# Summing the two column sets of the last half tile one behind the other, and storing the first during the second

## The chip, the cores and the metric

The kernel runs on one NeuronCore of a Trainium2 chip. The metric is the time of one execution on the device, in microseconds. Before the change the median of three runs is 351.83 us (351.61 to 352.06). A profile is one further execution, recorded by the hardware profiler: its span runs from the first to the last recorded instruction, and its own time is the span and what lies around it.

Names of engines: PE (matrix products), DVE and ACT (vector and scalar work, both used here for copies out of PSUM), POOL and SP (here they only issue DMAs and pass signals on). SP, ACT and POOL each have a queue of their own for DMAs; DMAs issued from SP and ACT have their descriptors made by hardware, those from POOL by software.

## The reference

Attention with normalised q and k, and a multiplicative feed-forward on its output. With x the attention's output, reshaped to 3584 tokens of 768 values:

```python
q_n, k_n = (rmsnorm(q, g_q), rmsnorm(k, g_k))
scores = scale * np.matmul(q_n, k_n.transpose(0, 1, 3, 2))
attn = np.exp(scores - np.max(scores, axis=-1, keepdims=True))
attn = attn / (np.sum(attn, axis=-1, keepdims=True) + 1e-09)
x = np.matmul(attn, v)                 # batch 8, heads 12, 448 positions, head size 64
a = x @ w1
b = x @ w2
h = a * b @ w3
out = h @ w_out                        # (3584, 768), float32
```

## The kernel before

The kernel multiplies w3 and w_out together once (`w34s`), so that the end of the feed-forward is a single product, (a * b) @ w34. Batches are taken in pairs, 896 tokens each, in seven tiles of 128 tokens; `abT` holds the transposed a * b of a pair, with 8 blocks of 128 rows (`CF` = 8). Six of the last pair's seven tiles are ordinary passes (`ffn2_pair`): 64x64 products into two PSUM banks, one copy of 128x768 into `half`, and two stores of 64 rows, for the last pair one from SP and one from ACT.

The last tile of all is different. `do_last` makes it in two halves of 64 tokens (x = 0, then x = 1). In a half, the 768 output columns are cut in four pieces of 192 (`w`): `nh` picks the left or right 384 columns and becomes the upper or lower 64 partitions of the result, `c` picks the first or second 192 of these and becomes the PSUM bank `z + c`. So one bank holds a column set: the piece `c` of both column halves. For each of the 8 blocks there are four matmuls of 192 columns (two sets, two halves), 32 in a half tile. In the kernel before, all four of a block come before the next block, so both banks are complete at the end. Then DVE copies bank `z` and ACT copies bank `z + 1` into a buffer that is free by then (`qk_bufs[0]`, called `qk_sb` in the profile), and when both are done, SP stores the left 384 columns of the 64 rows and ACT the right ones (96 KB each).

The order of everything is made by a planner (`Planner`). It is a simulation in Python: each operation is a `Job` with a cost, a key and conditions for when it may start; the planner takes the earliest job, emits its instruction, and so fixes the order in each engine's queue. The numbers in `add(...)` (an engine, an estimated cost, a key, `needs`) and the times `at` are the planner's own estimates: they set the order of emission, not when an instruction runs. What runs when is set by semaphores, which the framework adds from the data that each instruction reads and writes. The framework also gives each DMA one of eight semaphores ("lanes") for hardware-made descriptors or one of eight for software-made ones; an issue first waits until the DMA that last used its lane has landed.

`hand_over` uses signals on SP or POOL between two parts of an accumulation; in the last 80 us these are the only instructions of POOL. At the end of the program (line 1426 in the profile) SP waits for every DMA semaphore, each engine drains, and the engines meet in a barrier that POOL leads.

Of the kernel before, what the change touches and what calls it, by code (L numbers as in the profile page):

```python
# [20 lines left out]
SEM = 0.05  # L21
TO_ENGINE = 0.23
TO_ENGINE_WIDE = 0.45
# [22 lines left out]
class Planner:  # L46
# [11 lines left out]
    def add(self, *args, **kw):  # L58
        self.jobs.append(Job(*args, **kw))
# [136 lines left out]
def kernel(  # L196
# [13 lines left out]
    nc = tc.nc  # L210
# [3 lines left out]
    HP = NP // 2  # L214
# [9 lines left out]
    CF = DFF // 128  # L224
    NH = DM // 2
# [50 lines left out]
    w34s = const.tile([128, CF, DM], BF, name="w34s")  # L276
# [43 lines left out]
    ps_all = psum.tile([NP, 8, 512], FP, name="ps_all")  # L320
# [9 lines left out]
    free, add = plan.free, plan.add  # L330
# [20 lines left out]
    xT, abT = {}, {}  # L351
# [11 lines left out]
    def copy_on(engine, out, in_, by=None):  # L363
        if engine == "ACT":
            nc.scalar.activation(  # L365
                out=out, in_=in_, func=AF.Copy, scale=1.0 if by is None else by
            )
        elif by is not None:
            nc.vector.tensor_scalar(out=out, in0=in_, scalar1=by, scalar2=None, op0=MULT)
        else:  # L370
            nc.vector.tensor_copy(out=out, in_=in_)  # L371
# [252 lines left out]
    def into(m):  # L624
        extra = DRAIN if mode[0] != m else 0.0
        mode[0] = m
        return extra

    def pass_us(n):
        return n / 2400 + 0.0025  # L630
# [421 lines left out]
    def out_rows(bp, t, x):  # L1052
        bb, j = divmod(2 * t + x, NJ)
        r0 = (2 * bp + bb) * S
        return out[r0 : r0 + S].rearrange("(p j) n -> j p n", j=NJ)[j]
# [9 lines left out]
    def do_last(t, z):  # L1065


        x = last_x[0]
        last_x[0] += 1
        bp, tl = B // 2 - 1, NT - 1  # L1070
        c0 = tl * 128 + HP * x
        w = NH // 2
        for fi in range(CF):
            for c in range(2):
                for nh in range(2):
                    n0 = nh * NH + c * w
                    nc.tensor.matmul(  # L1077
                        out=ps_all[HP * nh : HP * nh + HP, z + c, 0:w],
                        lhsT=abT[bp][:, fi, c0 : c0 + HP],
                        rhs=w34s[:, fi, n0 : n0 + w],  # L1080
                        start=(fi == 0), stop=(fi == CF - 1),
                        tile_position=(0, HP * nh), skip_group_check=True,
                    )
        took = 2 * CF * pass_us(w) + into("l")
        bank_at[z] = bank_at[z + 1] = INF
        spare = qk_bufs[0].rearrange("p w x j d -> p (w x j d)")
        o_sb = spare[:, x * NH : (x + 1) * NH].rearrange("p (z n) -> p z n", z=1)
        ends = []

        def store(nh):  # L1090
            eng = nc.scalar if nh else nc.sync
            eng.dma_start(
                out=out_rows(bp, tl, x)[:, nh * NH : (nh + 1) * NH],
                in_=o_sb[HP * nh : HP * nh + HP, 0],
            )

        def done(e):
            ends.append(e + SEM)
            if len(ends) == 2:
                for nh in range(2):  # L1100
                    add(
                        "ACT" if nh else "SP", 0.6, -500.0 + nh,
                        lambda nh=nh: store(nh), needs=[lambda: max(ends)],
                    )

        for c, (e, us) in enumerate((("DVE", 0.27), ("ACT", 0.25))):
            add(
                e, us, -500.0,
                lambda e=e, c=c: copy_on(
                    e, o_sb[:, 0, c * w : (c + 1) * w], ps_all[:, z + c, 0:w]  # L1110
                ),
                needs=[lambda: t + took + TO_ENGINE_WIDE - 0.16], done=done,
            )
        return took

    def push_ffn(b):
# [137 lines left out]
    def pe_try(t, r):  # L1254
# [47 lines left out]
        if next_pv[0] == NQ and not waiting and not pairs and last_x[0] < 2 and two is not None:  # L1302
            if tile_at(B // 2 - 1, NT - 1) + SEM <= r:
                return do_last(t, two)
# [10 lines left out]
    with tc.manual_schedule():  # L1315
# [41 lines left out]
        def spread():  # L1357
# [14 lines left out]
            done=lambda t: consts_at.update(g=t + SEM) or bank_at.__setitem__(6, t + SEM),  # L1372
# [9 lines left out]
        for name in POOL_ORDER:  # L1382
            what, x = name[0], int(name[1])
# [9 lines left out]
            else:  # L1393
                dst, src, key = (w1s, moe_w1, "w1") if what == "a" else (w2s, moe_w2, "w2")
# [36 lines left out]
```

## Time and profile before

| | us |
|---|---|
| median of three runs | 351.83 |
| lowest, highest | 351.61, 352.06 |
| profiled execution, its own time | 351.65 |
| its span | 349.7 |
| PE busy in the span | 342.6 (98%) |
| ACT busy | 259.9 (74%) |
| DVE busy | 210.2 (60%) |
| POOL busy | 76.8 (22%) |
| last matmul ends (by the chain of waits) | 345.7 |
| last store issued | 346.14 |

The granted PE clock is 0.999 throughout. Times in the profile count from the start of the span. "Line op out<-in" names a group by the line of the kernel that made it and by the tiles that it writes and reads; L371 and L365 are the lines of the copy helper on DVE and ACT, L1077 is the matmul of `do_last`, L1092 its stores, L1018 the stores of the ordinary last tiles, L420 the loads of v from POOL, and L881 the ordinary passes. "Idle before <-" gives how long an engine stood idle before an instruction and what it waited for. Engines with a q (SPq, ACTq, POOLq) are the engines' queues: issues of DMAs and waits there don't count as busy time.

### The profile page before, as it was taken

What the parts mean: (1) busy time and instruction counts of PE and PEld (TensorE: products, weight loads), DVE (VectorE), ACT (ScalarE), POOL (GpSimd) and SP (SyncE); (2) the same over time, 40 slices, a digit from 0 to 9 for tenths busy, and PEclk for the clock granted to TensorE, in tenths of its full rate; (3) what the DMA queues carried; (4) which work ended last, traced back from release to release, by engine and by line L of the source; (5) the groups of instructions that cost most, each with busy time, mean ns of one, the idle gap of its engine ahead of it and who ended that gap; (6) DMA issues with size and microseconds to landing.
All of it is one profiled execution on the core that took longest, in us unless ns stands there. A gap on an engine that the chain in (4) does not pass through costs nothing.

```text
span 349.7 us, 16194 instructions
## 1 busy us (share of the span) xinstructions
PE 342.6 (98%) x7374; PEld 221.3 (63%) x7374; DVE 210.2 (60%) x296; ACT 259.9 (74%) x372; POOL 76.8 (22%) x134
## 2 busy tenths in 40 slices
PE   8999999999999999999999999999999999999995
PEld 4766656657665766656666575676665656666674
DVE  5379377997989679986669678575633221222100
ACT  4779979979999999998699898667876842222122
POOL 8376720204020520132050111403130000000000
PEclk9999999999999999999999999999999999999999
DMA  8999999589999997984998789834590014000054
GB/s 194 235 283 192 233 300 253 108 174 260 187 232 216 176 260 178 222 220 62 217 248 175 169 135 265 182 54 64 113 167 8 4 47 116 27 2 2 4 170 150
DMA packets 68488, 55.11 MB, mean 158 GB/s; under 512 B 45060, under 2 KB 62372, under 8 KB 68420
## 3 DMA queue, kind: packets, MB, share of 16 engines
q1 hardware_dynamic: 49440, 35.33, 43.3%
q0 software_dynamic: 18048, 16.92, 27.8%
q10 hardware_dynamic: 932, 1.84, 1.4%
q8 instruction: 57, 0.93, 1.1%
q14 instruction: 11, 0.09, 0.1%
HBM read 46.66 MB, written 11.01 MB: 165 GB/s over the span
## 4 chain that ended last, share of the span: by engine, by line
PE 85%; ACT 8%; DVE 3%; issue 2%; DMA 1%; ACTq 0%; SPq 0%
PE ps_all L881 62%; PE ps_all L779 12%; PE ps_all L692 8%; ACT P L714 3%; PE ps_all L758 2%; ACT half L714 1%; ACT Pr L714 1%; DVE qks L507 1%; ACT sq L477 1%; DMA qk_sb<-in_q_dram 1%; PE ps_all L1077 1%; PE ps_all L1136 1%; DVE w34s L371 1%; ACT w_outs L714 1%; ACT w34s L365 0%
## 5 line engine op out<-in xcount | busy, mean ns | idle before, releaser
L714 ACT ACTIVATE P<-ps_all 128x896 bf16<-128x896 f32 x114 | 99.9, 918 | 11.0 <-PE ps_all L692 10.5
L420 POOL DMA_DIRECT2D v_sb<-in_v_dram x96 | 57.2, 623 | 175.9 <-PE ps_all L692 93.0
L881 PE MATMUL ps_all<-xT,w1s 64*64 64x448 bf16 x1536 | 88.1, 349 | 0.0
L881 PE MATMUL ps_all<-xT,w2s 64*64 64x448 bf16 x1536 | 87.3, 349 | 0.0
L881 PE MATMUL ps_all<-w34s,abT 64*64 64x384 bf16 x1728 | 80.6, 323 | 0.0
L365 ACT ACTIVATE half<-ps_all 128x896 bf16<-128x896 f32 (+1 forms) x35 | 30.7, 877 | 50.2 <-PE ps_all L881 50.2
L962 DVE TENSOR_TENSOR abT<-ps_all,half 128x896 bf16<-128x896 f32 x32 | 34.8, 1088 | 51.5 <-PE ps_all L881 49.9
L881 PEld LDWEIGHTS <-abT 64*64 64x64 bf16 x1728 | 52.8, 107 | 19.0 <-issue 0.4
L881 PEld LDWEIGHTS <-w2s 64*64 64x64 bf16 x1536 | 46.6, 107 | 25.3
L881 PEld LDWEIGHTS <-w1s 64*64 64x64 bf16 x1536 | 46.5, 107 | 25.2
L692 PE MATMUL ps_all<-qkT 64*64 64x448 bf16 x672 | 60.6, 352 | 0.6 <-DVE abT L962 0.3
L484 DVE TENSOR_REDUCE ssq<-sq 128x14 f32<-128x896 f32 (+1 forms) x50 | 51.0, 1040 | 12.8 <-ACT sq L477 12.8
L507 DVE TENSOR_TENSOR qks<-qk_sb,al 128x448 bf16<-128x448 f32 x96 | 55.7, 617 | 2.9 <-ACT al L496 2.8
L477 ACT ACTIVATE sq<-qk_sb 128x896 f32<-128x896 f32 (+1 forms) x50 | 45.2, 920 | 1.8 <-DMA qk_sb<-in_q_dram 1.5
L821 DVE TENSOR_TENSOR xT<-ps_all,r 128x448 bf16<-128x448 f32 x48 | 27.5, 616 | 13.5 <-ACT r L802 9.9
L692 PEld LDWEIGHTS <-qkT 64*64 64x64 bf16 x672 | 22.0, 106 | 14.2 <-issue 5.1
L881 PE MATMUL ps_all<-w_outs,w3T 64*64 64x384 bf16 x512 | 25.1, 323 | 0.8 <-DVE w3T L371 0.5
L779 PE MATMUL ps_all<-P,v_sb 128*32 128x448 bf16 x456 | 25.3, 352 | 0.0
L714 ACT ACTIVATE w_outs<-ps_all 128x896 bf16<-128x896 f32 x24 | 21.2, 917 | 3.8 <-PE ps_all L692 3.6
L779 PEld LDWEIGHTS <-v_sb 128*32 128x32 bf16 x592 | 16.1, 97 | 12.5 <-issue 0.8
L714 ACT ACTIVATE Pr<-ps_all 128x896 bf16<-128x896 f32 x24 | 22.2, 924 | 1.0 <-PE ps_all L692 0.9
L371 DVE COPY half<-ps_all 128x768 f32<-128x768 f32 x14 | 13.4, 957 | 13.9 <-PE ps_all L881 11.3
(65 smaller groups left out, 215.2 us busy)
## 6 DMA issues: line engine op xcount, KB each, us to landing
out_dram<-half SPq DMA_DIRECT2D x48, 192.0 KB, 3.8
qk_sb<-in_q_dram SPq DMA_DIRECT2D x15, 448.0 KB, 4.8
qk_sb<-in_k_dram SPq DMA_DIRECT2D x15, 448.0 KB, 5.6
v_sb<-in_v_dram POOLq DMA_DIRECT2D x48, 64.0 KB, 4.5
v_sb<-in_v_dram POOLq DMA_DIRECT2D x48, 48.0 KB, 4.6
qk_sb<-in_q_dram POOLq DMA_DIRECT2D x5, 448.0 KB, 11.9
qk_sb<-in_k_dram POOLq DMA_DIRECT2D x5, 448.0 KB, 12.2
w3s<-in_moe_w_dram POOLq DMA_DIRECT2D x8, 256.0 KB, 6.7
```

The source lines that it names most:

```text
L365: nc.scalar.activation(out=out, in_=in_, func=AF.Copy, scale=1.0 if by is None else by)
L371: nc.vector.tensor_copy(out=out, in_=in_)
L420: nc.gpsimd.dma_start(out=v_bufs[i % 4][p0 : p0 + HP, g::2, 0 : j1 - j0].rearrange("p h j d -> p h (j d)"), in_=src[:, g::2, j0:j1].rearra ...
L477: nc.scalar.activation(out=s["sq", t][:, x0:x1], in_=src[:, t, x0:x1], func=AF.Square)
L484: nc.vector.tensor_reduce(out=s["ssq"][:, t, x0:x1], in_=s["sq", t][:, x0:x1], axis=AX, op=ADD)
L507: nc.vector.tensor_tensor(out=s["qks"][:, t, :, x], in0=src[:, t, x], in1=s["alpha"][:, t, x].unsqueeze(2).broadcast_to([NP, NJ, D]), op=MULT,
L692: nc.tensor.matmul(out=sc[HP * c : HP * c + HP, u, 0:S].rearrange("p (j s) -> p j s", j=NJ), lhsT=qkT[u * D : (u + 1) * D, 1, j, cols], rh ...
L714: lambda: nc.scalar.activation(out=dst, in_=sc[:, :, 0:S], func=AF.Exp),
L779: nc.tensor.matmul(out=ps_all[hd * HALF : (hd + 1) * HALF, z, 0:S], lhsT=value_weights(i, hd, j, kind), rhs=s["P"][:, hd, j, :] if j < NF ...
L821: lambda: nc.vector.tensor_tensor(out=xT[b][:, 2 * m + kind - 1, :], in0=ps, in1=s["r"], op=MULT),
L881: mm = nc.tensor.matmul(out=ps_all[64 * h : 64 * h + 64, p.bank + z, 0 : p.n], lhsT=lhsT[64 * r : 64 * r + 64, 64 * h : 64 * h + 64], rhs= ...
L962: nc.vector.tensor_tensor(out=abT[bp][:, f0 : f0 + 2, odd * S : (odd + 1) * S], in0=ps_all[:, z : z + 2, 0:S], in1=a_sb[b, f0], op=MULT,)
```

## The change

Only `do_last` changes, and only for the second half (x = 1). The 32 matmuls are sorted by column set: 16 for `c = 0` over all 8 blocks, then 16 for `c = 1`. The copies and stores are made by a new function `finish`, called once per group of columns. For x = 0 it is called once, with both copies and the same two stores as before. For x = 1 it is called twice: the first set is copied by DVE and stored from SP (left part) and POOL (right part); the second set is copied by ACT and stored from SP and ACT. Each of the four stores has 64 rows of 192 columns, 48 KB. The planner's time `at` of the first set is earlier by the time of 8 of the 16 pairs.

```diff
-        for fi in range(CF):
-            for c in range(2):
-                for nh in range(2):
...
+        steps = [(fi, c) for fi in range(CF) for c in range(2)]
+        for fi, c in sorted(steps, key=lambda y: y[1]) if x else steps:
+            for nh in range(2):
...
-        def store(nh):
-            eng = nc.scalar if nh else nc.sync
+        def store(nh, n0, n1, eng):
             eng.dma_start(
-                out=out_rows(bp, tl, x)[:, nh * NH : (nh + 1) * NH],
-                in_=o_sb[HP * nh : HP * nh + HP, 0],
-            )
...
+                out=out_rows(bp, tl, x)[:, nh * NH + n0 : nh * NH + n1],
+                in_=o_sb[HP * nh : HP * nh + HP, 0, n0:n1],
+            )
+
+        def finish(n0, n1, parts, at, queues):
+            ends = []
+
+            def done(e):
+                ends.append(e + SEM)
+                if len(ends) == len(parts):
+                    for nh, (name, eng) in enumerate(queues):
+                        add(
+                            name, 0.6, -500.0 + nh,
+                            lambda nh=nh, eng=eng: store(nh, n0, n1, eng),
+                            needs=[lambda: max(ends)],
+                        )
+
+            for e, us, m0, m1 in parts:
+                add(
+                    e, us, -500.0,
+                    lambda e=e, m0=m0, m1=m1: copy_on(
+                        e, o_sb[:, 0, m0:m1], ps_all[:, z + m0 // w, m0 % w : (m1 - 1) % w + 1]
+                    ),
+                    needs=[lambda: at], done=done,
+                )
+
+        at = t + took + TO_ENGINE_WIDE - 0.16
+        ends_on = (("SP", nc.sync), ("ACT", nc.scalar))
+        if x:
+            finish(0, w, (("DVE", 0.27, 0, w),), at - CF * pass_us(w), (ends_on[0], ("POOL", nc.gpsimd)))
+            finish(w, NH, (("ACT", 0.25, w, NH),), at, ends_on)
+        else:
+            finish(0, NH, (("DVE", 0.27, 0, w), ("ACT", 0.25, w, NH)), at, ends_on)
         return took
```

More of the change, by code (lines that the diff above doesn't have):

```diff
@@ L1072, in do_last @@
         w = NH // 2
-        for fi in range(CF):
-            for c in range(2):
-                for nh in range(2):
[L1076 to L1082, printed above, removed]
-                    )
+        steps = [(fi, c) for fi in range(CF) for c in range(2)]
+        for fi, c in sorted(steps, key=lambda y: y[1]) if x else steps:
+            for nh in range(2):
+                n0 = nh * NH + c * w
+                nc.tensor.matmul(
+                    out=ps_all[HP * nh : HP * nh + HP, z + c, 0:w],
+                    lhsT=abT[bp][:, fi, c0 : c0 + HP],
+                    rhs=w34s[:, fi, n0 : n0 + w],
+                    start=(fi == 0), stop=(fi == CF - 1),
+                    tile_position=(0, HP * nh), skip_group_check=True,
+                )
         took = 2 * CF * pass_us(w) + into("l")
@@ L1087, in do_last @@
         o_sb = spare[:, x * NH : (x + 1) * NH].rearrange("p (z n) -> p z n", z=1)
-        ends = []
-        def store(nh):
-            eng = nc.scalar if nh else nc.sync
+        def store(nh, n0, n1, eng):
             eng.dma_start(
-                out=out_rows(bp, tl, x)[:, nh * NH : (nh + 1) * NH],
-                in_=o_sb[HP * nh : HP * nh + HP, 0],
-            )
[L1097 to L1113, printed above, removed]
+                out=out_rows(bp, tl, x)[:, nh * NH + n0 : nh * NH + n1],
+                in_=o_sb[HP * nh : HP * nh + HP, 0, n0:n1],
+            )
```

## The prediction

> **What bounds the kernel now.** I read the page first (span and busy shares), then the chain that ended last, and then the last ten microseconds, since all edits lie there. PE is busy 98% of the span; nothing in the change adds or takes a matmul, and the reordered ones are the last on PE. So only the tail after PE can move. The chain of waits over the end:
>
> ```profile
> 4 pieces in order of time: start us, us, what
> 335.93 6.99 PE ps_all L881 x172
> 342.92 2.78 PE ps_all L1077 x64
> 345.70 0.01 issue
> 345.71 0.36 DVE qk_sb L371
> ```
>
> It ends in a copy at 346.07, yet the span is 349.7: 3.6 us follow in which no compute engine works. The timeline of the end says what starts there (start, duration, engine; an SPq or ACTq row is an issue):
>
> ```profile
> 342.85 2.83 PE L1077 MATMUL ps_all<-w34s,abT 128*64 128x192 bf16 x64
> ...
> 344.39 0.36 DVE L371 COPY qk_sb<-ps_all 128x192 f32<-128x192 f32 x1 [15.86 <-PE ps_all L1077]
> 344.52 0.33 ACT L365 ACTIVATE qk_sb<-ps_all 128x192 f32<-128x192 f32 x1 [0.58 <-PE ps_all L1077]
> ...
> 345.71 0.36 DVE L371 COPY qk_sb<-ps_all 128x192 f32<-128x192 f32 x1 [0.96 <-PE ps_all L1077]
> 345.72 0.33 ACT L365 ACTIVATE qk_sb<-ps_all 128x192 f32<-128x192 f32 x1 [0.87 <-PE ps_all L1077]
> 346.14 0.49 ACTq L1092 DMA_DIRECT2D out_dram<-qk_sb  x1
> ```
>
> The last issue is at 346.14. The DMA answer for 340 to 349.7 gives 2.4 us to landing for SP's last store and 2.6 for ACT's: the end of data is 346.14 + 2.61 = 348.75. Then comes the program's own ending, line 1426:
>
> ```profile
> L1426 SPq EVENT_SEMAPHORE  x12: 17/28/28, 346.6 to 349.7; - x12
> L1426 POOLq EVENT_SEMAPHORE  x4: 17/17/17, 349.0 to 349.6; - x4
> L1426 POOLq DRAIN  x3: 46/101/2518, 340.5 to 349.5; - x3
> L1426 ACTq DRAIN  x2: 8/316/625, 346.7 to 349.2; - x2
> ```
>
> SP waits for all DMA semaphores (until 348.83), drains, and signals; POOL collects the engines' signals at 348.995 and 0.75 us of barrier follow to 349.75. The reader should see the third row: POOL drains three times, and the first, at 340.45, lasted 2.518 us. Today it is over at 342.97, six microseconds before POOL is needed. How full the DMA engines are in between:
>
> ```profile
> 346.20:347.40 1.20, 0.00 (x0) 0.00 (x0) 0.00 (x0) 0.00 (x0) 0.00 (x0) 1.00 0.76 272
> 347.40:348.30 0.90, 0.00 (x0) 0.00 (x0) 0.00 (x0) 0.00 (x0) 0.00 (x0) 1.00 0.68 208
> ```
>
> The last but one number is the DMA share: 0.76, then 0.68. So the end is set by latency from the last issue, with some queueing.
>
> **What the skill says.** (1) The Trainium skill, "PSUM — Partial Sum Buffer", Terms: two engines must not touch the same bank and quadrant at once. The two column sets lie in banks z and z+1, so the first may be copied while the second is summed. The trace agrees for other banks: the copies at 344.39 and 344.52 run while PE sums the next half. (2) "DMA: Bandwidth & Descriptors", Issuing engines are not separate DMA queues: stores of SP, ACT and POOL share 16 engines and interleave, so a third queue brings no bandwidth. (3) The same page, Specifications: first byte about 1 us after a software-generated (POOL) issue, 0.6 for SP and ACT. In the trace the first packets of the last SP store begin at 347.4, 1.25 us after the issue's start, 0.8 after its end; POOL's v loads in quiet stretches (issues at 236.9, 252.2, 258.6) show 1.3 to 2.0 us from the start. It agrees that POOL is slower. (4) "Perfetto Trace Analysis", Sequencer-only Instruction: a DRAIN's recorded time begins when its waits are met. So the 2.518 us is execution, not a wait. No page says what POOL does in it.
>
> **The change part by part.**
>
> *Order of sums.* 32 matmuls stay 32, with the same 32 weight loads. Pairs start every 0.0825 us in the trace of before. The first set's last pair moves from the 15th place to the 8th, 7 x 0.0825 = 0.58 us earlier; the second set's last stays where it is. Cost nothing, within 0.02 us: consecutive pairs now add into one bank, and line 881 already runs at full rate with two matmuls in one bank behind each other.
>
> *DVE copy of the first set.* Moves from 345.71 to 345.13, ends 345.49. DVE has nothing else. SP's queue has the store of the first half ahead (344.88 to 345.34), over by then.
>
> *First-set stores, two new issues.* SP: wait, then start 0.065 us after the copy as today (346.066 to 346.130), so 345.555 to 346.02 (0.467 us). That is 0.1 us before SP is needed again at 346.12; if it were later, the second store would slip by the excess, at most 0.05. POOL: in the trace's records POOL's issues whose DMA-lane semaphore came last start 0.284 us after it (thirteen cases, 0.283 to 0.290). So 345.49 + 0.285 = 345.77, and with the v loads' 0.595 us, done at 346.37. Landing is not shown for a POOL store. Low end: the fastest v load, 2.2 us, 347.97; high end: 2.9 us as at 252.2, 348.7; I take 2.6, 348.4.
>
> *Second-set copy and stores.* ACT copies at 345.72 as today, done 346.05; both stores wait for it alone instead of for two copies. Issues at 346.12, 0.015 earlier. Their size halves: 64 packets of 768 B each instead of 1,536. By the packet records, 3,072 B takes 121 ns and 1,536 B 65, so 768 B is estimated at 37: 128 x (65 - 37) / 16 = 0.22 us less work behind the last issue. In all it is 256 x 37 against 128 x 65: 0.07 us more, which with the first-set packets (2 x 0.15 us) must fit in the idle 24% of 346.2 to 347.4, 0.29 us. So 0 to 0.1 us carries over. Bounds of the gain: 0 (latency alone counts: 192 KB stores have landed in 2.5 us too) and 0.35; I take 0.25. End of data 348.5, SP ready at 348.7 instead of 348.96.
>
> *POOL's ending.* POOL's first closing DRAIN stands behind its new DMA: not at 340.45 but at 346.37 + 0.08 = 346.45 (0.08 was the gap at 340.37). With its 2.518 us it ends at 348.97, and POOL collects signals at about 349.0, against 348.995 today. The cover is gone to the last 0.03 us: what DMA gains, this DRAIN gives back. Bounds: if it is short here (the others are 0.05 and 0.10 us), it costs nothing; if it first waits for POOL's own store to land at 347.97 to 348.7 and then runs its 2.518, it ends at 350.5 to 351.2.
>
> Sum on the profiled execution: 351.65 us is 349.7 of span and 1.95 around it. SP's path -0.25, POOL's path +0.00, and the later of them counts: 349.0 - 348.995, about 0.0, so 351.65 again. The median of the three runs is 0.18 above this; added to it, the forecast is 351.8.
>
> **Rivals.**
>
> *The gain comes through* (POOL's DRAIN short, or a fixed task counted from somewhere else): the end is SP's at 348.7 and 351.83 - 0.25 = 351.6. For it: two DRAINs of 0.05 and 0.10 us on the same engine, and the one at the program's start, 0.18. Against it: those come with no DMA of POOL since the one before, the 2.518 us one does. More than 0.7 us of gain would need a landing 1.5 us after the issue, where no store shows under 2.4.
>
> *POOL's end waits for its store* (the slower side): the DRAIN sees an open software-generated transfer, holds until it has landed, and only then does its 2.518 us. From 348.995 to 350.5 or 351.2: +1.5 to +2.2 us, 353.3 to 354.0. It decides from the point where the DRAIN ends after 349.7, which is an execution of 3.3 us. For it: the only long DRAIN is the first after POOL's DMAs. Against: at 340.45 POOL's last transfer was 79 us old, so those 2.518 us can't have been such a wait.
>
> *The copy isn't early* (the DVE copy still waits for the last matmul): POOL issues at 346.07 + 0.285, DRAIN 347.0 to 349.55, +0.55 us, 352.4. Against: before, DVE starts 0.13 us ahead of ACT at 344.39, so each copy waits for its own bank.
>
> **How the numbers follow.** What a measurement of this kernel can tell from no change is about 0.2%, 0.7 us. Likeliest (a tie of the two paths): 0.50, own range 351.4 to 352.3 (the DMA and DRAIN bounds of 0.35 each way, and the runs' 0.2). Gain through: 0.20, still within 0.2%. POOL waits for its store: 0.20, slower. Copy not early: 0.05, within. The rest, 0.05: a larger gain than any row explains. To those within 0.2% I leave 0.70: 0.05 of the likeliest goes to slower, for a DRAIN some 0.8 us longer than today's. Faster 0.05, same 0.70, slower 0.25. The range must reach into the slow case to leave out no more than 2 in 10: 351.3 to 353.5.
>
> **What would show it.** In the profile after: one DVE copy near 345.1 and one ACT copy near 345.7; SP issues near 345.55 and 346.12; a POOL issue near 345.8; SP's last wait for a landing near 348.5; POOL's long DRAIN from 346.4, its first signal event at 349.0. A POOL DRAIN of 0.1 us and an end at 349.45 shows the first rival; one past 350, the second; a DVE copy at 345.7, the third. I am wrong on DMA if the last landing stays at 348.75 though the stores are halved.

## The result and the profile after

The changed kernel takes 353.33 us (median of 12 runs, 352.12 to 354.45), the kernel before 351.62 in the runs beside it: a ratio of 1.0041, 95% interval 1.0027 to 1.0055 (the two medians alone give 1.0049). It is slower, where a tie was forecast. In a second comparison (after_again below, 22 runs against 68, on one chip) it is 1.0025 (1.0010 to 1.0039).

The profiled execution took 353.76 us with a span of 352.0, against 349.7 before: 2.2 us more. Two things have to be kept apart. I call *tail* the time from the first matmul of the last tile (L1077) to the end of the span; times in the tail are counted from that matmul. Before, it starts at 342.85, so the tail is 6.90 us. After, from the timeline of the end (start, duration, engine, line):

```profile
344.30 2.83 PE L1077 MATMUL ps_all<-w34s,abT 128*64 128x192 bf16 x64
...
346.33 1.77 SPq L1090 DMA_DIRECT2D out_dram<-qk_sb  x3
...
346.59 0.36 DVE L371 COPY qk_sb<-ps_all 128x192 f32<-128x192 f32 x1 [0.39 <-PE ps_all L1077]
347.18 0.33 ACT L365 ACTIVATE qk_sb<-ps_all 128x192 f32<-128x192 f32 x1 [0.87 <-PE ps_all L1077]
347.24 0.56 POOL L1090 DMA_DIRECT2D out_dram<-qk_sb  x1 [84.81 <-PE ps_all L1077]
347.54 0.50 ACTq L1090 DMA_DIRECT2D out_dram<-qk_sb  x1
```

The tail is 7.68 us, 0.78 more. The other 1.45 us are lost before the last tile, where the instructions of PE are the same in both programs. In the table by stretches of time the first large loss shows between 139 and 147 us (the columns are the stretch, its length, the busy time of PE, PEld, DVE, ACT and POOL with the number of instructions, the granted clock, the DMA share and GB/s). The first line is of the kernel before, the second of the kernel after:

```profile
139.00:147.00 8.00, 8.00 (x184) 5.41 (x174) 7.14 (x11) 7.97 (x12) 2.38 (x4) 1.00 1.15 260
```

```profile
139.00:147.00 8.00, 7.09 (x152) 4.56 (x148) 6.04 (x9) 6.86 (x11) 2.38 (x4) 1.00 0.99 191
```

PE lost 0.91 us there, 200 us before the first changed instruction, with less DMA traffic (191 GB/s for 260). Such losses differ from run to run: over all the profiles of this study, in which the PE program up to the last tile is the same, that tile starts between 342.47 and 345.06 us. They are noise for this question, and the tail is what can be compared to a few hundredths of a microsecond: three profiles with the stores of the change have tails of 7.68, 7.73 and 7.71 us.

In the tail, the rows of the program's own ending (line 1436 after, 1426 before) and the chain of waits:

```profile
L1436 SPq EVENT_SEMAPHORE  x12: 17/28/1681, 348.1 to 351.9; - x12
L1436 POOLq EVENT_SEMAPHORE  x4: 17/17/17, 351.2 to 351.9; - x4
L1436 POOLq DRAIN  x3: 46/98/3967, 347.2 to 351.7; - x3
L1436 SPq DRAIN  x3: 7/7/7, 350.7 to 351.4; - x3
```

```profile
342.06 5.16 issue
347.22 0.58 POOLq L1436
```

The chain no longer ends in a DVE copy but in POOL's ending. POOL's first closing drain begins at 347.22, together with its issue at 347.24, and lasts 3.967 us: until 351.18. SP, which waits for all stores, is done with its waits and ready to signal at 350.80, so everybody waits 0.4 us for POOL. The stores (queue, number, size, median us from issue to landing):

```profile
out_dram<-qk_sb SPq DMA_DIRECT2D x2, 48.0 KB, 2.7
out_dram<-qk_sb POOLq DMA_DIRECT2D x1, 48.0 KB, 2.6
out_dram<-qk_sb ACTq DMA_DIRECT2D x1, 48.0 KB, 2.6
```

Stores of half the size land no sooner after their issue than the 2.4 and 2.6 us of before. So there are two questions: what POOL's drain waits for, and where the gain of the smaller stores went.

### The profile page after: what moved, and what is told of

It is laid out like the page before. It is cut to its first block, busy times and chain, and to the rows that moved or that the text cites. A ratio compares the mean times of both kernels' runs of the same rounds, so it can differ in the third digit from the quotient of the medians.

```text
span 352.0 us, 16199 instructions
## 1 busy us (share of the span) xinstructions
PE 342.6 (97%) x7374; PEld 219.5 (62%) x7374; DVE 210.3 (60%) x296; ACT 260.2 (74%) x372; POOL 77.4 (22%) x135
## 4 chain that ended last, share of the span: by engine, by line
PE 76%; ACT 11%; DVE 4%; issue 4%; DMA 3%; SPq 0%; POOLq 0%; DVEq 0%; ACTq 0%
PE ps_all L881 55%; PE ps_all L779 11%; PE ps_all L692 7%; ACT P L714 5%; DMA qk_sb<-in_k_dram 2%; PE ps_all L758 2%; DVE qks L507 2%; ACT sq L477 2%; ACT half L714 1%; ACT Pr L714 1%; DMA qk_sb<-in_q_dram 1%; PE ps_all L1146 1%; DVE w34s L371 1%; ACT w_outs L714 1%; DVE xT L821 0%
```

## The experiments

Theory A: the loss sits in the tail, and POOL's ending behind its store sets it. Rivals: the changed order of sums or copies costs time itself; the program is slower before the tail; the drain takes a fixed time from the issue, whatever the store does. Times finer than 0.1 us are read from the trace's records of instructions and of semaphores. Where no ratio is given, the kernel ran once, and only its tail is read.

**The change again.**

> The changed kernel as it is. The tail is the time from the first matmul of the last tile to the end of the span: 6.9 us before, 7.7 us in the first profile after. Theory A (the loss sits in the tail, in POOL's ending and SP's waits): tail 7.6 to 7.8 again, and the time about 0.8 us above before; what lay above that in the first result (1.45 us earlier in the run) is chance and changes. Rival (the changed program also runs slower before the tail): the last tile starts 1 us or more later than before again, and the time is 1.4 us or more above.

Ratio 1.0025 (1.0010 to 1.0039), that is 0.9 us (the medians are 0.7 us apart). The last tile starts at 342.66, even 0.19 earlier than before, so the loss ahead of it is not part of the change. The tail is 7.73. POOL's drain in this run:

```profile
L1436 POOLq DRAIN  x3: 46/98/4019, 345.6 to 350.1; - x3
```

It is 0.05 us longer than in the first profile, and its store landed 0.05 later (5.61 against 5.56).

**Order and early copy alone.** `finish` is called once, as for x = 0:

```diff
-            finish(0, w, (("DVE", 0.27, 0, w),), at - CF * pass_us(w), (ends_on[0], ("POOL", nc.gpsimd)))
-            finish(w, NH, (("ACT", 0.25, w, NH),), at, ends_on)
+            finish(0, NH, (("DVE", 0.27, 0, w), ("ACT", 0.25, w, NH)), at, ends_on)
```

> Sums sorted by column set and the first set copied early, but both stores of the second half at the end as before (96 KB each, SP and ACT, no POOL). Theory A: no loss, tail 6.9, ratio 1.000 within 0.001. Rival (the new order of the sums slows PE, or the early copy disturbs it): tail longer by 0.2 us or more, and the second set's copy later than 2.87 us after the first matmul of the tile.

Ratio 1.0001 (0.9988 to 1.0014), tail 6.87. The first set is copied at 2.28, as in the change, and the second at 2.87, as before. The new order of sums and the copies cost nothing; the stores do.

**POOL alone, in the kernel before.** The right store of one half goes to POOL:

```diff
-            eng = nc.scalar if nh else nc.sync
+            eng = (nc.gpsimd if x == 1 else nc.scalar) if nh else nc.sync
...
```

(`...` stands for the planner's own name of that engine, changed in the same way.)

> The kernel before with one edit: the right store of the second half (96 KB) is issued from POOL instead of ACT. If the program's end stands behind POOL's store (it lands, then 1.3 us of POOL's drain): issue 3.5 us after the tile's first matmul, landing near 6.1, drain over near 7.4, tail 8.1 to 8.2, time +1.2 to +1.3 us (ratio 1.0035). If POOL is harmless: tail 6.9 to 7.1.

Ratio 1.0045 (1.0031 to 1.0060), tail 8.19. POOL's drain (row of the program's ending) and the store:

```profile
L1426 POOLq DRAIN  x3: 46/98/3591, 346.3 to 350.4; - x3
```

```profile
out_dram<-qk_sb POOLq DMA_DIRECT2D x1, 96.0 KB, 2.2
```

POOL issued at 3.82, later than I had worked out (3.5), and the store landed at 6.07; the drain was over at 7.39. POOL waits for two copies here and starts 0.60 us after the later one; in the change it waits for one and starts 0.29 us after it. What a second wait does on POOL was not tried. One store moved to POOL costs 1.3 us, more than the whole change.

The same with `x == 0`, a store issued 1.3 us earlier:

> The kernel before with the right store of the first half (96 KB), not of the second, issued from POOL. POOL starts near 2.3 us after the tile's first matmul. If the drain ends 1.3 us after the landing (2.7 us after the start): over near 6.3, about where SP is ready (6.1), so tail 7.0 to 7.2, a loss of 0.1 to 0.3 us. If POOL is harmless: tail 6.9 or a little less, since ACT has one store less.

Tail 7.55: worse than expected, since POOL started at 2.51 and its store landed only at 5.43. The drain ended at 6.75, after SP at 6.14. Even the first half of the last tile is too late for POOL.

**What the drain waits for.** A load into an unused buffer is added at the end of POOL's queue, early enough that its drain is over long before the end, once 16 KB and once 448 KB (there the added line is `load_qk(1, 0, nc.gpsimd)`):

```diff
         plan.run(pe_step, finished)
+        nc.gpsimd.dma_start(out=qk_bufs[1][0:HP, 0, 0, 0, :], in_=q[0, 0, 0:HP, :])
```

> The kernel before with a load of 16 KB added at the end of POOL's queue, where it runs near 340.5 us, far from the end, into a buffer that nobody uses any more. It measures POOL's first closing drain after a short transfer. If the drain waits for the landing and then takes 1.3 us (as after: landing 349.86, drain over 351.18): its end is 1.3 us after the landing, some 3.5 us after the load's start. If it runs a fixed time from the end of the issue (3.4 us after): its end is 3.4 us after the issue's end. Time as before.

> The same with a load of 448 KB. The issue takes about as long, the landing is later by 1.5 us or more. If the drain waits for the landing: its end moves with the landing, again 1.3 us after it. If it is a fixed time from the issue: its end stays 3.4 us after the issue's end, whatever the landing.

Here the load lands in 2.0 and in 3.7 us. The answers on DMAs and the rows of POOL's drain, first the small load, then the large one:

```profile
qk_sb<-in_q_dram POOLq DMA_DIRECT2D x1, 16.0 KB, 2.0
...
L1427 POOLq DRAIN  x3: 46/107/3381, 343.0 to 351.3; - x3
```

```profile
qk_sb<-in_q_dram POOLq DMA_DIRECT2D x1, 448.0 KB, 3.7
...
L1427 POOLq DRAIN  x3: 46/107/5003, 342.6 to 351.1; - x3
```

The drain grows by 1.62 us, the time from issue to landing also by 1.62. A fixed time from the issue is ruled out: from the end of the issue it is 2.81 us in one and 4.24 in the other. (The small load leaves the tail at 6.86; the large one delays the stores behind it, tail 7.03, though POOL's drain is over at 3.26.) Over all seven profiles with a POOL DMA open at the end, the drain is over 1.32 us after its landing:

| run | landing | drain over | difference |
|---|---|---|---|
| after | 5.559 | 6.879 | 1.320 |
| after_again | 5.611 | 6.931 | 1.320 |
| pool_last | 6.068 | 7.388 | 1.320 |
| pool_first | 5.427 | 6.748 | 1.321 |
| probe_small | 0.293 | 1.614 | 1.321 |
| probe_large | 1.940 | 3.261 | 1.321 |
| after_lanes (below) | 5.584 | 6.905 | 1.321 |

With no POOL DMA for 79 us, the drain takes 2.518 us from its own start, in all seven profiles of that kind. What it does in that time was not tried.

**What half the size is worth.** The first set is copied but not stored, so only the two stores of 48 KB follow:

```diff
-            finish(0, w, (("DVE", 0.27, 0, w),), at - CF * pass_us(w), (ends_on[0], ("POOL", nc.gpsimd)))
+            finish(0, w, (("DVE", 0.27, 0, w),), at - CF * pass_us(w), ())
```

> The order of sums and the copies of the change, but the first column set of the last 64 rows is not stored at all (that part of the output is left out), and only the two stores of 48 KB of the second set follow. It measures what half the size is worth at the end. If the last landing is set by the bytes: SP's and ACT's stores land 0.2 us or more sooner after their issue than the 2.45 and 2.61 us of before. If it is set by latency and the number of packets (64 per store in both): within 0.1 us of before.

The landings of the second set's stores:

```profile
out_dram<-qk_sb SPq DMA_DIRECT2D x1, 48.0 KB, 2.2
out_dram<-qk_sb ACTq DMA_DIRECT2D x1, 48.0 KB, 2.4
```

2.19 and 2.36 us after issues at 3.23, against 2.47 and 2.64 in order_only with issues at the same time and 96 KB: 0.28 us sooner each. Tail 6.58. So half the size alone is worth, in this place, what I had put on it, 0.25 us.

Then the left part of the first set is stored from SP, the right part left out (no POOL store):

> The changed kernel without the store from POOL: the right part of the first set of the last 64 rows is left out of the output. Without POOL's drain the tail is SP's: with its waits in the order of the change 0.57 us after the last landing. If the first set's SP store delays only its own queue: SP's last store lands 2.5 us or more after its issue (2.70 in the change, 2.19 with no first set stored), ACT's 2.36 as with none. If the shared engines are the limit, both are 0.1 to 0.2 us late. Tail 7.0 to 7.1.

```profile
out_dram<-qk_sb SPq DMA_DIRECT2D x2, 48.0 KB, 2.6
out_dram<-qk_sb ACTq DMA_DIRECT2D x1, 48.0 KB, 2.3
```

(The 2.6 is the median of SP's two.) SP's last store lands 2.51 us after its issue, 0.32 later than without the first set; ACT's after 2.33, not later at all. SP's own early store takes back SP's gain, and the packet records show how. SP's queue has packets under way all the time in between: the first set's store is issued at 2.67, but its packets begin only at 4.23, while those of the first half's store still run, and the second set's begin at 4.80, as the first set's end (4.82). With no first set stored they begin at 4.36. The tail is 7.11, since SP is ready only 0.58 us after the last landing, of which more below. In the change, with POOL's store too, it is 2.70 and 2.64 (2.81 and 2.76 in after_again): POOL's store costs another 0.2 to 0.3 us on SP and 0.3 to 0.4 on ACT. Nothing of the 0.28 is left. The added bytes alone don't explain SP's part: in no_pool, the next experiment, the same bytes go out from ACT instead of POOL, and SP's last store lands after 2.50, as here. Why POOL's queue weighs more was not tried.

**The change without POOL.** The right part of the first set goes out from ACT, and DVE copies the second set:

```diff
-            finish(0, w, (("DVE", 0.27, 0, w),), at - CF * pass_us(w), (ends_on[0], ("POOL", nc.gpsimd)))
-            finish(w, NH, (("ACT", 0.25, w, NH),), at, ends_on)
+            finish(0, w, (("DVE", 0.27, 0, w),), at - CF * pass_us(w), ends_on)
+            finish(w, NH, (("DVE", 0.27, w, NH),), at, ends_on)
```

> All four stores of 48 KB as in the change, but the right part of the first set issued from ACT instead of POOL, and the second set copied by DVE since ACT issues then. If POOL's ending alone made the loss: SP's path has the gain that was forecast, tail 6.65. If SP's path lost too (in the profile after, SP was ready 6.50 us after the tile's first matmul, 6.11 before): tail 7.2 to 7.3, still 0.3 to 0.4 above before and 0.4 below the change.

Ratio 1.0017 (1.0003 to 1.0031), tail 7.31: still 0.41 slower than before. The last landing is at 5.96, as in the kernel before (5.90) within 0.06, but SP is ready 0.57 us after it, not 0.21. SP works through a fixed list of waits at the end, two semaphores per entry, about 0.06 us each. In this kernel there are four hardware-made stores of the second half, in the change three, instead of two before. The semaphores are given out in turn, so the store that lands last now has one in the third of the ten entries, and seven entries are still to be read when it lands, where before it was one. To test it, six loads of 32 bytes on SP, in the middle of the run, turn the semaphores by six (added to this kernel):

```diff
+        if b == 3:
+            for n in range(6):
+                nc.sync.dma_start(out=g_row[:, 0, 8 * n : 8 * n + 8], in_=g_q[8 * n : 8 * n + 8].unsqueeze(0))
```

> The kernel of no_pool, with six loads of 32 bytes added on SP's queue in the middle of the run (they write a row that is no longer used), so that the DMA semaphores go round by six and the last two stores get the two that SP waits for last at the end. In no_pool SP was ready 0.57 us after the last landing, before 0.21. If the order of SP's waits makes the 0.36: 0.21 here, and the tail 6.9 to 7.0 instead of 7.31. If it is the number of stores: 0.57 and 7.3 again.

SP's waits without and with the turn (engine, line, waited for: us in total, times, longest):

```profile
SPq L1436 <- DMA out_dram<-qk_sb: 2.0, 1, 2.0
```

```profile
SPq L1439 <- DMA out_dram<-qk_sb: 1.0, 3, 0.5
SPq L1439 <- PEq L1439: 0.7, 2, 0.5
SPq L1439 <- DMA out_dram<-half: 0.6, 1, 0.6
```

One wait of 2.0 us for a late store, with the rest of the list behind it, has become waits in the order in which the stores land. The last landing is at 5.90, SP is ready at 6.11, the tail 6.89. The order of the list is worth 0.36 us (0.21 from landing to ready, where it was 0.57). And this is the early store without POOL and without that penalty: it equals the kernel before (6.90), no more.

The same turn (by seven) in the change itself:

> The changed kernel with seven such loads, so that its last stores get the last two semaphores of SP's waits. SP should be ready 0.36 us earlier, near 6.2 instead of 6.5 after the tile's first matmul. If POOL's drain alone sets the end, the tail stays 7.7. If SP's path counts too, it is shorter by up to 0.36.

SP is ready at 6.21 instead of 6.50, and the tail is 7.71, unchanged: in the change it is POOL alone that sets the end, and SP's loss lies hidden under it.

**A version that might beat both.** order_only, with the second set's copy split:

```diff
+            m = w + w // 2
+            finish(0, NH, (("DVE", 0.27, 0, w), ("DVE", 0.2, w, m), ("ACT", 0.2, m, NH)), at, ends_on)
```

> An attempt at a version that beats both: sums sorted by column set, the first set copied early by DVE, the second set's copy split between DVE and ACT (96 columns each), and then the two stores of 96 KB from SP and ACT as before. The copy of 192 columns takes 0.33 to 0.36 us; with half the columns 0.25 is expected, so stores 0.08 to 0.13 us earlier than before and the tail 6.75 to 6.85. Ratio 0.9997, within what the runs can tell of 1.

Ratio 0.9992 (0.9977 to 1.0007), tail 6.82. The expected step failed:

```profile
347.39 0.25 ACT L365 ACTIVATE qk_sb<-ps_all 128x96 f32<-128x96 f32 x1 [0.87 <-PE ps_all L1077]
347.68 0.26 DVE L371 COPY qk_sb<-ps_all 128x96 f32<-128x96 f32 x1 [0.52 <-ACT qk_sb L365]
```

DVE waits for ACT, though it copies other columns. Both read the same bank here, while the copies of the first half, from two banks, overlap (1.54 to 1.90 on DVE, 1.67 to 2.00 on ACT); that the bank is the reason is likely, but was not tried. The stores are issued at 3.44, 0.16 later than before. That the tail is 0.08 shorter all the same goes with the stores ahead of them, which landed 0.09 sooner in this run. So the time to landing isn't a fixed latency: these 96 KB stores land 2.14 and 2.38 us after their issue, those of order_only, issued 0.21 earlier, after 2.47 and 2.64. By the packet records SP's last store moves in 0.66 us here and in 0.87 there, where it starts beside the stores of the first half. No version here beats the kernel before by more than the runs can tell.

## Why the prediction was wrong

*Order of sums and copies: right.* 2.28 and 2.87 us after the first matmul, as worked out (345.13 and 345.72 less 342.85), at no cost (order_only, 1.0001).

*POOL's issue and store: right.* The issue was put 2.92 us after the tile's first matmul with a landing 2.6 later; it came at 2.93 and landed after 2.62. The 2.6 had been picked between 2.2 and 2.9 us, so that it fits to 0.02 us is luck.

*POOL's ending: the step that failed.* I took the 2.518 us of the kernel before as a fixed execution and laid it behind the end of the issue, giving 6.12 and a tie with SP. It ends 1.32 us after the landing, at 6.88. These 0.76 us are all but 0.02 us of the error in the tail. I leaned on the Trainium skill, "Perfetto Trace Analysis", Sequencer-only Instruction, by which a DRAIN's recorded time begins when its semaphore waits are met, and concluded that the time is not a wait. The trace names no semaphore that this drain waits for; but the recorded 3.967 us, begun 0.02 before POOL's own DMA, contain the wait for that transfer. The rival with a chance of 0.20 named this mechanism, and was too pessimistic by a full 1.2 us: it added the 2.518 to the landing, where the remainder is 1.32. My argument against it, that those 2.518 us can't have been such a wait, was true and said nothing about what happens with a transfer open.

*Second set's stores: a term sized right, its give-back too small.* Half the size is worth 0.28 us (0.25 forecast; a packet of 768 bytes takes 36 ns, 37 estimated). I let 0 to 0.1 us carry over from the first set's stores by adding up packet times against idle DMA time, and the 0.07 us of that sum already held the first set's packets, which were then counted again. It still came out too small: against the kernel with no first set stored it is 0.51 us on SP in the change (2.70 for 2.19) and 0.29 on ACT (2.64 for 2.36), 0.32 of SP's from its own first store. The DMA engines had room on average (the stretch that was 0.76 busy before, 3.35 to 4.55 us after the first matmul, is 0.85 busy after), but SP's second store stood behind its first in its own queue: its packets begin at 4.85 in the change, as the first's end (4.86). By the prediction's own sign it was wrong on DMA: the last landing stayed, 5.93 for 5.90. Two readings were off, though nothing hangs on them: the packets of SP's last store before begin at 347.28 at the latest, 1.15 us after its issue, not 1.25; and of the three stretches called quiet for POOL's loads, those at 252 and 258 are not (DMA share 0.86 and 1.03, against 0.64 at 237).

*SP's list of waits: not thought of.* SP was put ready at 5.85 us; it is ready at 6.50, 0.28 us of the difference from the landing and the rest from the list. More hardware-made stores shift the store that lands last to a semaphore early in the list: 0.36 us between last landing and signal. It doesn't decide the change, but it would have turned a change without POOL into a loss too.

*The time.* 353.33 lies within the range, 351.3 to 353.5, because it reached for the slow rival; the likeliest case, a tie, was wrong. That it also falls on the low end of the rival's 353.3 to 354.0 is luck: the rival put 1.5 to 2.2 us on POOL's ending, which cost 0.78. The tail explains 0.78 to 0.83 us, 0.22 to 0.24%. The second comparison's 0.25% agrees with that. The first one's 0.41% is above it by about 0.65 us; the later start of the last tile in the first profile is of that kind, but was not seen again in after_again. What makes it differ between runs was not tried and stays open.

## What to carry to other kernels

Before moving a late transfer to another queue, price that queue's closing as well: a drain that was long over before can become the end of the program, and its length before says little about its length behind an open transfer. A store cut in two paid nothing here, as its first piece was still in the queue ahead of the second; so look at what the queue holds before counting on an early piece and a smaller last one. When the end of a program is a list of waits, look which of them the last transfers get: here it was worth 0.36 us that the list asked for them last.

## What was not expected of the hardware

- POOL's first closing drain ends 1.320 to 1.321 us after the landing of POOL's last DMA, in seven profiles, for stores and loads of 16 to 448 KB; with none open it takes 2.518 us.
- Behind the same stores, a store of 64 rows of 768 bytes lands 0.28 us sooner than one of 64 rows of 1,536 bytes; but with two of them from SP, issued 0.56 us apart, the second is 0.32 us later.
- Where SP and ACT issue two stores each within a microsecond (no_pool), an issue on ACT took 0.75 us instead of 0.50, and ACT's second one started 0.26 us after SP's. With the large load just landed one took 0.84 us. What lengthens an issue was not tried.
